# Retention, routed experts and a second MLP on one core: VectorE's steps beside the experts emitted later, and a weight conversion with two outputs

## The chip, the cores and the metric

The kernel runs on one NeuronCore of a Trainium2 chip. TensorE (PE; PEld is its weight load) does the matrix products and transposes, VectorE (DVE) and ScalarE (ACT) work element by element, GpSimd (POOL) issues gathers and scatters and large copies, SyncE (SP) issues the other DMAs. Each engine works through its own list of instructions in the order in which the program emitted them, and waits on semaphores for the others. The metric is the device time of one execution in microseconds (us), as the median of several.

## The reference

Three stages follow one another. The weights of the last stage come as 64-bit numbers.

```python
scores = scale * np.matmul(q, k.transpose(0, 1, 3, 2))        # 8 batches, 8 heads, 576 x 64
ret = scores * Dmat[None, :, :, :]                            # gamma ** (i - j) below the diagonal
x = np.matmul(ret, v)  ...  .reshape(4608, 512)

logits = x @ w_gate                                           # 8 experts, each takes 576 tokens
for idx in np.argsort(-logits.flatten()):
    tok, e = (int(idx) // E, int(idx) % E)
    if assigned[tok] >= 0 or counts[e] >= cap:
        continue
    assigned[tok] = e
    counts[e] += 1
for e in range(E):
    out[mask] = np.maximum(x[mask] @ w1[e], 0.0) @ w2[e]      # 512 -> 1024 -> 512

h = x @ w_in                                                  # 512 -> 2048 -> 512, all 4608 tokens
g = h * np.clip(h + 3.0, 0.0, 6.0) / 6.0
out = g @ w_out
```

## The kernel before

**Stages.** The retention stage and the logits come first, and the routing of the first expert follows. From 187.8 us on `mlps` runs two MLPs as one stream of TensorE work: the experts (eight times 576 tokens, in two halves of 288), then the second MLP (12 blocks of 384 tokens). The experts are filled one after the other: routing `r` finds which expert is full next and which 576 tokens it takes, by eight counting steps, a sort and a decoding.

**Arithmetic.** Every operand is split into a high and a low part, so that a product is three matmuls (`mm3`). For each weight, each token column and each hidden value there is thus a copy to the high part on ScalarE and a subtraction for the low part on VectorE. In an expert's half, unit `f` has 12 matmuls of the first layer (`A`, into one of two PSUM buffers `h`) and 12 of the second (`Bm`); `A(u+2)` is emitted ahead of `Bm(u)`. An expert is 384 matmuls. Unit `A(u+2)` writes the PSUM buffer that ScalarE (L724) and VectorE (L725) read for `A(u)`, and 36 matmuls lie between.

**What sets the order.** The order is written by the program itself. `mm3` calls `tick` after each matmul, and `tick` lets the side jobs go on that were started with `spawn`; a side job emits some instructions and says with `yield n` after how many further matmuls it wants to go on. The numbers are those of `PARAMS`. The side jobs are
- `route`: the next routing. In each counting step VectorE compares (L367, tile `cmp`), TensorE counts (L373), ScalarE copies (L377, `gs`), TensorE adds up (L382), VectorE tests (L385, `ge`), TensorE sums the flags (L389). At the end a sort (L456, L461) and a decoding that gives the list of tokens (L504, `idx`), with `self.routed` counted up behind it; the next routing begins at once (L510 to L367).
- `weights`: gathers w1 and w2 of the known expert (L530, issued by POOL) and splits them (L544 on ACT, twice L549 on DVE).
- `xload`: gathers the token rows (L567, issued by POOL), transposes them on TensorE (L592, PSUM bank `tp`, five pieces for each expert) and splits them (L596, L597). `w_xg` is how many matmuls lie between the issue of the first gather and its transposes.
- `convert`: turns the 64-bit weights of the second MLP into high and low parts. It goes through 32 pieces of 128x512 numbers: a load by SP (L615, one buffer `c_raw`), seven steps on VectorE (L633 to L657) and three on ScalarE (L642, L645, L653), and a store to HBM by SP (L620). All pieces write the same output buffer `self.cvo` (a part of `big`), and the store of piece `i-1` is emitted with the fourth step of piece `i`, one step ahead of L652, which writes the buffer again.
- `w2load`: brings the converted weights back, 2 MB at a time, into the buffers of the expert weights that are free (L672, issued by POOL).
- `yload`: brings the experts' results (stored by SP, L745) to the second MLP.

Before a unit of TensorE is emitted, `need_x`, `need_w` and `run_until` make the side jobs emit all that this unit reads.

## Time and profile before

| | us |
|---|---|
| median of 3 runs (1524.6 to 1533.34) | 1532.13 |
| the profiled execution | 1529.34 |
| its span | 1527.6 |
| PE busy, PEld busy | 1440.0, 1316.4 |
| DVE busy, ACT busy, POOL busy | 701.8, 530.9, 232.4 |
| experts, from 187.8 to 716.3 | 528.5 |

The profiled execution is 1.7 us longer than its span, the part that the instructions' records don't cover. Busy time alone says little here: VectorE is busy for 46% of the span, but it has its work between 150 and 720 us and little after that.

### The profile page before, as it was taken

Reading aid. Unit: us, or ns where it says so; the run is one execution under the profiler, and the core shown is the slowest. Engines: PE = TensorE matmul, PEld = TensorE weight load, DVE = VectorE, ACT = ScalarE, POOL = GpSimd, SP = SyncE. Lnnn points to the kernel's source line nnn. Section 1 sums busy time; section 2 is a strip of 40 time slices with the busy share of each in tenths; the row PEclk is TensorE's granted clock in tenths of the full one; section 3 lists DMA queues with packets and bytes.
Section 4 is the critical chain, followed back from the end, with each engine's and each line's share of the span. In section 5 each row is a group of like instructions: output and inputs, shape, how many; then the busy total and the mean of one; then the engine's idle time right before and its main releaser. Section 6 shows DMA issues by size and latency. Waiting matters only on the chain.

```text
span 1527.6 us, 27247 instructions
## 1 busy us (share of the span) xinstructions
PE 1440.0 (94%) x11270; PEld 1316.4 (86%) x11270; DVE 701.8 (46%) x1723; ACT 530.9 (35%) x1033; POOL 232.4 (15%) x260
## 2 busy tenths in 40 slices
PE   6898598889999899989999999999999999999998
PEld 5677488888989889989899999999999999999997
DVE  3344577678778686754232323233232323323222
ACT  3233343443434435533232323233232323323222
POOL 6860212121131122100000000000000000000000
PEclk9999798999999999999999999999999999999999
DMA  9981734455454457668410101000010100000000
GB/s 360 380 316 51 244 102 143 134 188 173 154 173 152 150 184 230 200 245 285 167 37 16 42 1 42 15 28 27 16 38 4 42 12 30 27 16 32 1 21 21
DMA packets 62988, 171.81 MB, mean 112 GB/s; under 512 B 7696, under 2 KB 22288, under 8 KB 61840
## 3 DMA queue, kind: packets, MB, share of 16 engines
q1 hardware_dynamic: 43568, 96.09, 18.1%
q0 software_dynamic: 16464, 70.26, 14.0%
q10 hardware_dynamic: 2832, 3.72, 0.7%
q8 instruction: 88, 1.44, 0.4%
q14 instruction: 36, 0.29, 0.1%
HBM read 124.96 MB, written 45.09 MB: 111 GB/s over the span
## 4 chain that ended last, share of the span: by engine, by line
issue 50%; PE 3%; POOL 3%; POOLq 0%; DVE 0%
POOL out_dram L790 2%; PE h L703 2%; PE y L703 1%; POOL nop L796 0%; POOLq L929 0%; POOL big L672 0%; POOLq L790 0%; POOL pair L672 0%; DVE hg L725 0%; POOLq L672 0%
## 5 line engine op out<-in xcount | busy, mean ns | idle before, releaser
L763 DVE SCALAR_TENSOR_TENSOR r<-r,h 128x384 f32<-128x384 f32 x192 | 106.4, 554 | 449.1 <-ACT r L762 449.1
L703 PE MATMUL h<-big,pair 128*128 128x288 f32 (+1 forms) x1440 | 281.6, 316 | 7.1 <-DVE hg L725 6.4
L762 ACT ACTIVATE r<-h,bias 128x384 f32<-128x384 f32 x192 | 111.5, 581 | 441.8 <-PE h L703 433.8
L703 PEld LDWEIGHTS h<-big,pair 128*128 128x128 f32 x1440 | 223.9, 194 | 10.3 <-DVE hg L725 6.7
L703 PE MATMUL h<-big 128*128 128x288 f32 (+1 forms) x864 | 188.6, 323 | 0.6 <-ACT big L596 0.6
L703 PE MATMUL y<-hg,pair 128*128 128x288 f32 x1056 | 172.3, 305 | 2.1 <-ACT r L744 2.1
L703 PE MATMUL h<-yact,big 128*128 128x384 f32 x768 | 173.4, 337 | 0.2 <-DVE r L763 0.2
L703 PE MATMUL h<-yact,pair 128*128 128x384 f32 x768 | 173.3, 337 | 0.0
L766 DVE TENSOR_TENSOR hg<-r,hg 128x384 fp32r<-128x384 f32 x192 | 107.3, 559 | 113.4 <-ACT hg L765 113.4
L703 PEld LDWEIGHTS y<-hg,pair 128*128 128x128 f32 x1056 | 150.3, 192 | 2.8 <-ACT r L744 2.4
L790 POOL DMA_INDIRECT out_dram<-xg,idx x36 | 35.1, 975 | 761.8 <-ACT xg L789 755.3
L780 PE MATMUL y<-pair,hg 128*128 128x512 f32 x576 | 148.9, 394 | 0.0
L780 PE MATMUL y<-big,hg 128*128 128x512 f32 x576 | 148.9, 394 | 0.0
L703 PEld LDWEIGHTS h<-yact,big 128*128 128x128 f32 x768 | 138.4, 188 | 6.9 <-DVE r L763 0.6
L703 PEld LDWEIGHTS h<-big 128*128 128x128 f32 x864 | 141.2, 194 | 3.3 <-ACT big L596 0.8
L703 PEld LDWEIGHTS h<-yact,pair 128*128 128x128 f32 x768 | 138.3, 188 | 6.1
L765 ACT ACTIVATE hg<-r 128x384 fp32r<-128x384 f32 x192 | 100.7, 524 | 119.1 <-DVE r L763 119.1
L530 POOL DMA_INDIRECT raw<-in_w_dram,widx x65 | 65.9, 1015 | 395.6 <-DMA xn<-raw 57.8
L780 PEld LDWEIGHTS y<-big,hg 128*128 128x128 f32 x576 | 106.7, 188 | 16.8
L780 PEld LDWEIGHTS y<-pair,hg 128*128 128x128 f32 x576 | 106.7, 188 | 16.6
L724 ACT ACTIVATE hg<-h 128x288 fp32r<-128x288 f32 x128 | 52.0, 409 | 115.6 <-PE h L703 111.1
L725 DVE SCALAR_TENSOR_TENSOR hg<-h,hg 128x288 fp32r<-128x288 f32 x128 | 58.2, 454 | 50.7 <-ACT hg L724 49.5
(171 smaller groups left out, 1766.6 us busy)
## 6 DMA issues: line engine op xcount, KB each, us to landing
qk<-in_qk_dram SPq DMA_DIRECT2D x36, 512.0 KB, 6.9
kv<-in_kv_dram SPq DMA_DIRECT2D x32, 512.0 KB, 7.1
c_raw<-in_w_dram SPq DMA_DIRECT2D x32, 512.0 KB, 4.0
w<-big SPq DMA_DIRECT2D x32, 512.0 KB, 4.9
yr<-yT SPq DMA_DIRECT2D x48, 192.0 KB, 2.3
pair<-w POOLq DMA_DIRECT2D x4, 2048.0 KB, 10.0
big<-w POOLq DMA_DIRECT2D x4, 2048.0 KB, 12.2
yT<-r SPq DMA_DIRECT2D x32, 144.0 KB, 3.9
```

The lines of the kernel that those rows point to most:

```text
L530: nc.gpsimd.indirect_dma_start(out=raw, out_offset=None, in_=a[("w1", "w2")[w]], in_offset=bass.IndirectOffsetOnAxis(ap=self.widx[:, r, g: ...
L703: self.nc.tensor.matmul(out, w, x, start=(first and i == 0), stop=(last and i == 2))
L724: nc.scalar.activation(h[:, 0], p, AF.Relu)
L725: nc.vector.scalar_tensor_tensor(h[:, 1], p, 0.0, h[:, 0].bitcast(F32), op0=OP.max, op1=OP.subtract)
L762: nc.scalar.activation(r, p, AF.Relu, bias=self.bias[:, 0:1])
L763: nc.vector.scalar_tensor_tensor(r, r, 6.0, p, op0=OP.min, op1=OP.mult)
L765: nc.scalar.activation(g[:, 0], r, AF.Copy)
L766: nc.vector.tensor_tensor(g[:, 1], r, g[:, 0].bitcast(F32), OP.subtract)
L780: nc.tensor.matmul(acc[b][t], g[:, gw, x], w[:, ww, c:c + 512], start=(f == 0 and i == 0), stop=(f == 15 and i == 2))
L790: ins = nc.gpsimd.indirect_dma_start(out=a["out"], out_offset=bass.IndirectOffsetOnAxis(ap=self.idx[:, 3 * b + t:3 * b + t + 1], axis=0), ...
```

## The change

The change has these parts (line numbers are those of the program before):
- **Steps behind their inputs.** VectorE's low part of a hidden value (L725) is put in a list (`later`) and emitted 5 matmuls after the ScalarE step that it reads. The low parts of token columns come `w_low` = 5 matmuls after ScalarE's, and VectorE's `ge` and the next `cmp` come `w_pe` = 2 matmuls after TensorE's steps that they read.
- **Spacing.** The first counting step of routings 2 to 7 has 34 matmuls between `cmp` and its use instead of 22 (`w_first` + 4 `add`); `add` is -1 instead of 0 for routings 0 and 1. Token pieces of experts 1 to 3 are emitted with 11 matmuls between one and the next for the first three (`w_xt0`), and expert 2's first transposes come 36 instead of 50 matmuls after the gather's issue (`w_xg` for `r` < 3).
- **Conversion.** It begins after routing 1 instead of at the start of the experts. It has two output buffers in turn, and the store is emitted right behind the last step of its piece. A piece has 7 times 17 matmuls (before 7 times 16) while routings go on, and 3 times 6 and 4 times 9 (before 7 times 10) after that. The order of the pieces is `CONV`; those of the first two eighths come last, and are written straight into two weight buffers that expert 6 was the last to use, without a store and a load.
- The decoding waits with `tp_x` until the token pieces under way have been read from the bank `tp`.

```diff
-PARAMS = dict(w_first=18, w_cmp=12, w_hop=7, w_hop2=8, w_pre=22, w_dec=16, w_add=1, w_t=2, w_load=40, w_gran=16, w_half=10, w_gran0=24,
-              w_xg=36, w_xg2=50, w_xt=40, w_cv=16, w_cv2=10, n_nat=12)
+PARAMS = dict(w_first=30, w_cmp=11, w_hop=5, w_hop2=7, w_pe=2, w_low=5, w_pre=22, w_dec=16, w_add=1, w_t=2, w_load=40, w_load0=60, w_gran=16, w_half=8, w_gran0=24, w_gran1=10,
+              w_xg=36, w_xg2=50, w_xt=40, w_xt0=4, w_cv=17, w_cv2=6, w_cv3=9, n_nat=12)
+CONV, DIRECT = (2, 3, 4, 5, 6, 7, 0, 1), 2
...
+    def later(self, n, do):
+        self.due.append([n, do])
...
     def tick(self, n=1):
+        for x in self.due:
+            x[0] -= n
+        while self.due and self.due[0][0] <= 0:
+            self.due.pop(0)[1]()
...
-            add = self.w_add if r > 1 else 0
+            add = self.w_add if r > 1 else -1
...
+                        if r:
+                            yield self.w_pe
                         ge = rw.tile([128, E], F16, name="ge")
...
+            while self.tp_x:
+                yield 1
             self.tp_busy = True
...
-                yield self.w_xg if r < 2 else self.w_xg2
+                yield self.w_xg if r < 3 else self.w_xg2
...
+            for src, d in parts:
                 nc.scalar.activation(d[:, 0], src, AF.Copy)
+            if r:
+                yield self.w_low
+            for src, d in parts:
                 nc.vector.tensor_tensor(d[:, 1], src, d[:, 0].bitcast(F32), OP.subtract)
...
-            yield self.w_xt
+            yield self.w_xt0 if r < 4 and j < 2 else self.w_xt
...
+        while self.routed < 2:
+            yield 1
+        nxt = issue(0)
         yield 30
+        for i, (g, w, hf) in enumerate(seq):
+            raw, o = nxt, self.cvo[i % 2]
+            if i >= direct:
+                while self.pB < (self.w2_old[g] // 4) * 16 + 8 + 2 * (self.w2_old[g] % 4) + 2:
+                    yield 1
+                o = self.pairs[SLOT[g]][:, w, :, hf * n:hf * n + n]
...
-            if i > first:
-                store(i - 1)
-            if i + 1 < last and self.cv_bufs == 1:
-                issue(i + 1)
-            yield pace()
-            o = self.cvo
+            if i + 1 < len(seq):
+                nxt = issue(i + 1)
+            yield pace(True)
...
             V.tensor_tensor(o[:, 1], t0.bitcast(F32), ta, OP.mult)
-            yield pace()
-        store(last - 1)
+            if i < direct:
+                nc.sync.dma_start(self.w32[g, :, w, :, hf * n:hf * n + n], o.bitcast(F32))
+            self.converted = i + 1
+            yield pace(True)
...
+    def need_w2(self, f, w):
+        k, direct = CONV.index(f // 2), len(CONV) - DIRECT
+        self.run_until("convert", lambda: self.converted >= (4 * k + 2 + 2 * w if k >= direct else 4 * k + 4))
+        if k < direct:
+            self.run_until("w2load", lambda: self.w2_ready > k)
...
-            nc.vector.scalar_tensor_tensor(h[:, 1], p, 0.0, h[:, 0].bitcast(F32), op0=OP.max, op1=OP.subtract)
+            self.later(self.w_low, lambda: nc.vector.scalar_tensor_tensor(h[:, 1], p, 0.0, h[:, 0].bitcast(F32), op0=OP.max,
+                                                                          op1=OP.subtract))
```

In the lists that follow, before and after, a line's number is that of its own program: L652, L657, L615, L620, L725, L745 of before are L671, L676, L639, L678, L747, L768 of the change.

The first place is SP's list from the end of expert 6 on, before. `w<-big` is the store of a converted piece, `c_raw` the load of the next, `yT` the experts' results.

```order
L620 DMA w_77<-big 128x2x512
L615 DMA c_raw<-in_w_dram 128x1024
L745 DMA yT<-r 128x288 x2
L745 DMA yT<-ys 128x288 x2
L620 DMA w_77<-big 128x2x512
L615 DMA c_raw<-in_w_dram 128x1024
L620 DMA w_77<-big 128x2x512
L615 DMA c_raw<-in_w_dram 128x1024
L620 DMA w_77<-big 128x2x512
L615 DMA c_raw<-in_w_dram 128x1024
L745 DMA yT<-r 128x288 x2
L745 DMA yT<-ys 128x288 x2
```

The same in the change, from the last store of a piece on.

```order
L678 DMA w_77<-big 128x2x512
L639 DMA c_raw<-in_w_dram 128x1024
L678 DMA w_77<-big 128x2x512
L639 DMA c_raw<-in_w_dram 128x1024
L768 DMA yT<-r 128x288 x2
L768 DMA yT<-ys 128x288 x2
L639 DMA c_raw<-in_w_dram 128x1024 x4
L768 DMA yT<-r 128x288 x2
L768 DMA yT<-ys 128x288 x2
L639 DMA c_raw<-in_w_dram 128x1024 x2
L768 DMA yT<-r 128x288 x2
L768 DMA yT<-ys 128x288 x2
```

The store stood behind the four result stores of a half expert and now stands ahead of them; the last eight pieces have no store, and their loads follow one another.

The second place is VectorE's list where routing 3 begins, before (`v`, `t`, `ky`, `K`, `oh` lead to the first `cmp`; `big<-c_ta` and `c_t` are the conversion).

```order
L341 TENSOR_REDUCE v<-L 128x36 [waits DVE_49]
L347 MEMSET cmp 128x32
L349 TENSOR_SCALAR t<-v 128x36 [waits DVE_49]
L652 SCALAR_TENSOR_TENSOR big<-c_ta,c_t_4156 128x512 [waits DMAHW6_49,Activation_49]
L352 TENSOR_TENSOR ky<-t,v 128x36 [waits DVE_49]
L354 TENSOR_SCALAR t<-ky 128x36 [waits DVE_49]
L356 CAST K_4351<-t 128x36 [waits DVE_49]
L357 TENSOR_SCALAR ky<-ky 128x36
L725 SCALAR_TENSOR_TENSOR hg<-h,hg 128x288 [waits Activation_49]
L359 TENSOR_TENSOR oh<-L,v 128x288
L361 CAST K_4360<-ky 128x36 [waits DVE_49]
L367 SCALAR_TENSOR_TENSOR cmp<-K_4351,cf 128x576
```

The same in the change.

```order
L353 TENSOR_REDUCE v<-L 128x36 [waits DVE_49]
L359 MEMSET cmp 128x32
L361 TENSOR_SCALAR t<-v 128x36 [waits DVE_49]
L364 TENSOR_TENSOR ky<-t,v 128x36 [waits DVE_49]
L567 TENSOR_TENSOR pair_2217<-raw,pair_2217 128x512 [waits DMASW3_49,Activation_49]
L366 TENSOR_SCALAR t<-ky 128x36 [waits DVE_49]
L368 CAST K_4300<-t 128x36 [waits DVE_49]
L369 TENSOR_SCALAR ky<-ky 128x36
L371 TENSOR_TENSOR oh<-L,v 128x288
L373 CAST K_4306<-ky 128x36 [waits DVE_49]
L379 SCALAR_TENSOR_TENSOR cmp<-K_4300,cf 128x576
```

L725 and L652 stood within the chain to `cmp`; now a weight split (L567) stands there, and L747 is behind `cmp`.

The third place is TensorE's list from the decoding of routing 2 on (which is the row ahead of the first one here), before; `h` and `y` are expert 1, `rt<-oh,cmp` the first count of routing 3.

```order
L703 MATMUL y_4219<-hg,big 128x288
L703 MATMUL y_4220<-hg,big 128x288 x3
L703 MATMUL y_4221<-hg,big 128x288 x3
L703 MATMUL y_4222<-hg,big 128x288 x3
L703 MATMUL h<-big,pair_2214 128x288 x12
L703 MATMUL y_4219<-hg,big 128x288 x3
L703 MATMUL y_4220<-hg,big 128x288 x3
L703 MATMUL y_4221<-hg,big 128x288 x3
L703 MATMUL y_4222<-hg,big 128x288 x3
L703 MATMUL h<-big,pair_2214 128x288 x12
L703 MATMUL y_4219<-hg,big 128x288
L373 LDWEIGHTS cmp
```

The same in the change, from the 34th matmul behind the decoding on.

```order
L725 MATMUL y_4187<-hg,big 128x288 x3
L725 MATMUL y_4188<-hg,big 128x288 x3
L725 MATMUL h<-big,pair_2214 128x288 x6
L610 MATMUL tp<-ident,xg 128x128 x4
L725 MATMUL h<-big,pair_2214 128x288 x6
L725 MATMUL y_4185<-hg,big 128x288 x3
L725 MATMUL y_4186<-hg,big 128x288 x2
L610 MATMUL tp<-ident,xg 128x128 x4
L725 MATMUL y_4186<-hg,big 128x288
L725 MATMUL y_4187<-hg,big 128x288 x2
L385 LDWEIGHTS cmp
L385 MATMUL rt<-oh,cmp 128x64
```

From the decoding to the first count there were 47 matmuls of the expert, and now there are 59; ahead of the count now stand two pieces of expert 2's token transposes (`tp<-ident,xg`), the first of them 45 matmuls behind the decoding.

## Rows read from the trace of the kernel before

**Rows 1.** Windows by expert: us, busy by engine, clock, DMA share, GB/s.

```profile
187.80:263.50 75.70, 68.20 (x561) 64.28 (x562) 54.91 (x167) 28.71 (x57) 15.24 (x15) 0.91 0.39 129
263.50:338.30 74.80, 65.23 (x570) 61.81 (x569) 53.39 (x159) 30.82 (x63) 14.69 (x15) 0.93 0.50 157
338.30:405.10 66.80, 62.35 (x567) 59.71 (x565) 52.26 (x158) 28.56 (x59) 13.65 (x14) 0.97 0.52 166
...
538.90:599.00 60.10, 57.49 (x447) 56.29 (x447) 48.23 (x158) 26.43 (x50) 18.49 (x18) 0.97 0.63 201
599.00:655.80 56.80, 54.67 (x402) 54.43 (x401) 39.99 (x78) 30.99 (x56) 10.58 (x11) 0.97 0.67 215
655.80:716.30 60.50, 54.09 (x387) 53.85 (x386) 28.79 (x56) 20.91 (x42) 2.16 (x5) 0.94 0.73 259
1000.00:1100.00 100.00, 100.00 (x503) 90.68 (x502) 30.32 (x56) 30.23 (x57) 3.25 (x6) 1.00 0.07 23
```

**Rows 2.** The waits of PE: us in total, times, longest.

```profile
PE rt L373 <- DVE cmp L367: 17.2, 11, 3.5
...
PE h L703 <- DVE hg L725: 6.4, 1, 6.4
...
PE rt L382 <- ACT gs L377: 4.9, 1, 4.9
...
PE tp L592 <- DMA xg<-xn,idx: 3.5, 2, 3.2
```

**Rows 3.** The timeline of DVE at three places: start, us, what, idle before.

```profile
277.35 0.69 DVE L652 SCALAR_TENSOR_TENSOR big<-c_ta,c_t 128x512 fp32r<-128x512 f32 x1 [5.80 <-DMA w<-big]
...
515.79 0.69 DVE L652 SCALAR_TENSOR_TENSOR big<-c_ta,c_t 128x512 fp32r<-128x512 f32 x1 [3.28 <-DMA w<-big]
...
673.01 0.69 DVE L652 SCALAR_TENSOR_TENSOR big<-c_ta,c_t 128x512 fp32r<-128x512 f32 x1 [9.70 <-DMA w<-big]
```

**Rows 4.** The timeline of SP ahead of the last of them.

```profile
659.39 0.88 SPq L745 DMA_DIRECT2D yT<-ys  x2
660.36 0.43 SPq L620 DMA_DIRECT2D w<-big  x1
```

**Rows 5.** All stores of the conversion (line L620).

```profile
DMA to landing us min/median/max: 2.7/4.9/12.6
```

**Rows 6.** The chain that ended last, after 675 us: start, us, what.

```profile
675.21 3.25 PE h L703 x12
678.46 2.23 PE y L703 x12
...
682.29 1.60 PE y L703 x12
```

**Rows 7.** The timeline where routings 3 and 4 begin.

```profile
315.55 0.22 DVE L504 SCALAR_TENSOR_TENSOR idx<-g,tp 128x4 int32<-128x4 f32 x2
...
319.78 0.74 DVE L367 SCALAR_TENSOR_TENSOR cmp<-K,cf 128x576 f16<-128x576 f32 x1
...
320.58 0.32 PE L373 MATMUL rt<-oh,cmp 128*128 128x64 f16 x5 [3.46 <-DVE cmp L367]
...
381.04 0.32 PE L373 MATMUL rt<-oh,cmp 128*128 128x64 f16 x5 [3.19 <-DVE cmp L367]
```

**Rows 8.** The timeline where expert 1's tokens come in.

```profile
243.65 0.35 DVE L504 SCALAR_TENSOR_TENSOR idx<-g,tp 64x1 int32<-64x1 f32 x2
...
248.79 0.63 PE L592 MATMUL tp<-ident,xg 128*128 128x128 f32 x4 [3.24 <-DMA xg<-xn,idx]
```

**Rows 9.** DVE by line in expert 6: busy us, mean ns, idle before.

```profile
L725 DVE SCALAR_TENSOR_TENSOR hg<-h,hg 128x288 fp32r<-128x288 f32 x17 | 7.8, 456 | 9.4 <-ACT hg L724 9.4
...
L657 DVE TENSOR_TENSOR big<-c_t,c_ta 128x512 fp32r<-128x512 f32 x6 | 4.1, 687 | 0.1
...
L640 DVE TENSOR_SCALAR c_t<-c_raw 128x512 int32<-128x512 int32 x6 | 2.5, 418 | 0.0
```

**Rows 10.** All loads of the conversion (line L615).

```profile
DMA to landing us min/median/max: 3.6/4.0/6.2
```

More of the change, by code (lines that the diff above doesn't have):

```diff
@@ L121, in step, with flush @@
             del self.side[name]
+    def later(self, n, do):
+        self.due.append([n, do])
+    def flush(self):
+        while self.due:
+            self.due.pop(0)[1]()
     def tick(self, n=1):
+        for x in self.due:
+            x[0] -= n
+        while self.due and self.due[0][0] <= 0:
+            self.due.pop(0)[1]()
         for name in list(self.side):
@@ L601, in xload, with convert @@
                     yield from issue(u)
-            yield self.w_xt
-    def convert(self, first, last):
+            yield self.w_xt0 if r < 4 and j < 2 else self.w_xt
+    def convert(self):
         nc, a, cv = self.nc, self.a, self.cv_p
@@ L608, in convert, with pace @@
         s0 = 0x38100000 / 2.0
-        raws = {}
-        seq = [(g, w, hf) for g in range(8) for w in range(2) for hf in range(2)]
+        seq = [(g, w, hf) for g in CONV for w in range(2) for hf in range(2)]
+        direct = 4 * (len(CONV) - DIRECT)
         def issue(i):
             g, w, hf = seq[i]
-            raw = cv.tile([128, n, 2], I32, name="c_raw", bufs=self.cv_bufs)
+            raw = cv.tile([128, n, 2], I32, name="c_raw")
             nc.sync.dma_start(raw, a["w64"][g, :, w, hf * n:hf * n + n].bitcast(I32).rearrange("p (n t) -> p n t", t=2))
-            raws[i] = raw
-        def store(i):
-            g, w, hf = seq[i]
-            nc.sync.dma_start(self.w32[g, :, w, :, hf * n:hf * n + n], self.cvo.bitcast(F32))
-            self.converted = i + 1
-        def pace():
-            return self.w_cv if "route" in self.side else self.w_cv2
-        issue(first)
-        yield 30
-        for i in range(first, last):
-            g, w, hf = seq[i]
-            raw = raws.pop(i)
+            return raw
+        def pace(late=False):
+            return self.w_cv if "route" in self.side else self.w_cv3 if late else self.w_cv2
+        while self.routed < 2:
+            yield 1
+        nxt = issue(0)
+        yield 30
+        for i, (g, w, hf) in enumerate(seq):
[4 more added lines that the diff above has]
+                o = self.pairs[SLOT[g]][:, w, :, hf * n:hf * n + n]
             lo, hi = raw[:, :, 0], raw[:, :, 1]
@@ L633, in convert @@
             V.tensor_scalar(t0, hi, 3, 0x3FFFF000, op0=OP.logical_shift_left, op1=OP.bitwise_and)
+            ta = cv.tile([128, n], F32, name="c_ta")
+            nc.scalar.activation(ta, hi, AF.Abs, bias=self.bias[:, 1:2])
             yield pace()
             V.scalar_tensor_tensor(t0, hi, -0x40000000, t0, op0=OP.bitwise_and, op1=OP.bitwise_or)
-            if i + 1 < last and self.cv_bufs == 2:
-                issue(i + 1)
+            nc.scalar.activation(ta, ta, AF.Abs, bias=self.bias[:, 2:3])
             yield pace()
@@ L657, in convert @@
             V.tensor_tensor(o[:, 1], t0.bitcast(F32), ta, OP.mult)
-            yield pace()
-        store(last - 1)
+            if i < direct:
+                nc.sync.dma_start(self.w32[g, :, w, :, hf * n:hf * n + n], o.bitcast(F32))
+            self.converted = i + 1
+            yield pace(True)
     def w2load(self):
-        old = (26, 27, 28, 29, 30, 31)
-        for g in range(8):
-            while self.converted < 4 * g + 4:
+        for k, g in enumerate(CONV[:len(CONV) - DIRECT]):
+            while self.converted < 4 * k + 4:
@@ L771, in Dm @@
             _, b, _, f = u
+            if b == 0:
+                self.need_w2(f, 1)
             w = self.pairs[SLOT[f // 2]][:, 1]
@@ L880, in run @@
                          for i in range(3)]
-            self.cvo = big[:, 15104:16128].rearrange("p (a b) -> p a b", a=2)
+            self.cvo = [big[:, 15104 + 1024 * i:16128 + 1024 * i].rearrange("p (a b) -> p a b", a=2) for i in range(2)]
             for name in ("xload", "w2load", "yload"):
```

41 lines of the change are left out of this document (18 added, 23 removed).

## The prediction

> **What bounds the kernel now.** I read the windows by expert first, then PE's waits, then the timeline on both sides of each long wait. The second MLP needs no reading beyond one row: between 1000 and 1100 us PE is busy all the time at full clock [rows 1], and the change leaves its instructions as they are. What can move lies in the experts, 528.5 us. There 12 matmuls take 1.60 us at full clock [rows 6], 0.133 us each, so the 384 of an expert take 51.2 us. The windows [rows 1] have 75.7 and 74.8 us for experts 0 and 1, 66.8 for expert 2 (3 and 4 are within 0.2 of it), 60.1, 56.8 and 60.5 for 5, 6 and 7. Some 8 us of each of the first five are the routing's own matmuls and the transposes, an estimate: expert 2 has 165 PE instructions more than expert 6 and is 10 us longer, waits included. The rest, some 75 us over all eight, is waiting, and PE at the lower of its two clocks (1.2 instead of 2.4 GHz) behind the waits: a mean clock of 0.93 over 74.8 us says that some 10 us ran at the lower one, and 0.97 says 4 us in each of the middle experts.
>
> PE waits mostly for VectorE [rows 2]: 17.2 us for the first count of a step (`cmp`), 6.4 once for a low part of `h`, 4.9 once for ScalarE's `gs`; 3.5 for gathered tokens. VectorE is busy for 52.3 of expert 2's 66.8 us [rows 1], and its list is strict, so what holds one step holds all behind it. Two things hold it. One is the store of the conversion: L652 writes the only output buffer and waited 5.80, 3.28 and 9.70 us for the store to land [rows 3]. The other is its own backlog where a routing ends and the next begins: in the 5 us behind `idx` at 315.55 it works without a pause and `cmp` comes at 319.78, while PE has waited 3.46 us for it [rows 7].
>
> **The change, part by part.**
>
> *Stores (term 1).* All three waits follow one pattern. The store is behind the four result stores on SP, and those wait for the expert's half to end: the result stores go out at 659.39, the piece's store at 660.36, and it lands 12.6 us later at worst [rows 4, 5]. PE's share of the three waits is 4.9 (behind `gs`), 1.9 (at 517 us, a part of the 17.2) and 6.4 us [rows 2], together 13.2. Behind the third the clock costs more: 24 matmuls took 3.25 and 2.23 us instead of twice 1.60 [rows 6], so 2.3 us. Expert 1 shows as much lost clock [rows 1], so I take the same 2.3 behind the first. After the change the store is ahead of the result stores, and the next piece writes the other buffer; L652 then waits for a store that is two pieces, 108 matmuls or 14.4 us, older, against 12.6 at worst. The last eight pieces have no store. Term 1 is -(13.2 + 4.6) = -17.8 us. Next late in these places is VectorE's ordinary backlog, which the change doesn't raise in the first two; bounds -8 (a third wait as long as the first comes back in expert 7) to -18.
>
> The Trainium skill ("DMA: Bandwidth & Descriptors", Anatomy of one DMA) gives a fixed 2.0 us and 436 GB/s for a transfer, an estimate of 3.2 us for a store of 512 KB. By that the store of 660.36 would have landed before L652 came to it, the second buffer would be worth some 2 us of PE's time, and the sum would end 16 us higher. The row's 9.70 us speaks against it here, so the sum keeps term 1.
>
> *Spacing of the first count (term 2).* The count stands 59 instead of 47 matmuls behind the decoding, 12 times 0.133 or 1.6 us. It can give that at each of four starts of a routing; two of the waits are 3.46 and 3.19 us [rows 7], and the 17.2 us less 1.9 leave 8.7 for the other two and the small ones. But expert 2's tokens take the place at the first of the four. In the trace tokens are transposed 4.8 us after the end of `idx` at the earliest (244.0 to 248.8) [rows 8], so with `idx` done at 315.8 not before 320.6, which is when PE goes on now. The first transposes now stand 36 matmuls, 4.8 us, behind the emission of `idx`, and PE passed that point at 312.1 (320.58 less the wait of 3.46, less 38 matmuls). It would come to them at 316.9 and wait 3.7. So the first start gives nothing. At the other three, tokens and count stand together 50 matmuls behind `idx`, and the wait falls by 1.6 each: 4.8. The clock fell behind each of them (0.97 of 67 us is 4 us, 2 us lost). Whether it still falls behind a wait of half the length no row here says: 0 to 1.7 each, and I take half of 5. Term 2 is -7.4, bounds 0 to -12.
>
> *Expert 0 (term 3).* Conversion starts after routing 1, so VectorE has three of its steps less in the stretch that ends with `idx` at 243.65: two of 0.68 and one of 0.42 [rows 9], some 1.6 us. PE's wait of 3.24 [rows 8] goes to 1.6. A clock of 0.91 over 75.7 us [rows 1] is 13.6 us at the lower level; the 4 at the start stay, the rest costs 4.8 now and I take half of it off. Term 3 is -4.0, bounds 0 to -8.
>
> *Steps behind their inputs.* VectorE stands idle 9.4 us before L725 in expert 6 alone [rows 9], waiting for ScalarE. With five matmuls between, other steps fill that. PE doesn't wait for these directly, so I count nothing; the gain shortens the backlogs of terms 2 and 3 and is what lets the bounds there reach further. The price: L725 must be done 36 matmuls or 4.8 us behind its unit, and 0.7 of that are now gone before it is emitted.
>
> *Denser conversion (term 4).* A piece is four steps of 0.68 us and three of 0.42 [rows 9], 4.0 us. After the routings it is spread over 54 instead of 70 matmuls, so expert 6 gets up to 1.6 pieces more, 6 us on a VectorE that is busy for 40.0 of 56.8 us [rows 1] and idle for ScalarE in most of the rest. If it fits in the idle time it costs nothing, if not 6; nearest is expert 2, where VectorE at 78% comes with a wait of 3.19 us [rows 7]. I take +3 for experts 5 to 7, bounds 0 to +8. The change also shifts two pieces from expert 0 to the end; expert 7 has the room, with 28.8 of 60.5 busy.
>
> *The load behind the result stores (term 5).* With one `c_raw`, the late pace leaves 36 matmuls, 4.8 us, between a load's issue and its first reader; loads land in 4.0 (3.6 to 6.2) us [rows 10]. Two loads of this stage are emitted 9 and 3 matmuls behind four result stores, which SP issues only after the half has ended, two of them in 0.88 us [rows 4]. VectorE then stands 3 us or so, twice, and 4.1 us of slack remain before PE feels it: +1, bounds 0 to +6.
>
> *Token pieces close together (term 6).* Experts 2 and 3 get their first three pieces 11 matmuls, 1.5 us, apart through one PSUM bank, while transposing (0.6) and two readers (0.6 each) take 1.8. Before, two of them were forced together anyway. +1.5, bounds 0 to +6.
>
> The two loads and eight stores of 2 MB eighths that fall away, and POOL's list, cost nothing, since PE waits for none of it now.
>
> **Sum.** -17.8 - 7.4 - 4.0 + 3 + 1 + 1.5 = -23.7. Against the profiled execution's 1529.34 that is 1505.6; the three runs shown lie from 1524.6 to 1533.3 with a median of 1532.1, 2.8 above it. I forecast 1506 us.
>
> **Rivals.**
> *The backlog takes it back.* VectorE remains as full as it is, PE's waits at the starts only change their names (tokens for count), the clock falls as before, and terms 4 to 6 come to half their upper bounds. Only the stores count: -17.8 + 9 (terms 4 to 6 to some 10 of 20) = -8.8, 1520 us. For it: VectorE at 78% through expert 2, and the tokens of expert 2 as worked out. Against: VectorE's 9.4 us of idle time that the later emission opens. Chance 0.22.
>
> *The waits are of one piece.* If a shorter backlog also keeps the clock up, experts 0 to 4 come near 62 us each (51.2, 8 and 3 for what waits remain). They take 351 us now, so that is -41; with -8.7 for the third store and terms 4 to 6 it makes -44, 1485 us. For it: the clock is lost only behind waits. Against: the tokens at 36 matmuls. Chance 0.15.
>
> *The last loads are late.* The direct pieces must be done when the second MLP reads them, with one `c_raw` in series: a piece takes a load and the 2.2 us up to its last read of `c_raw`. The last three loads run while the 2 MB copies fill the DMA engines. At 6.2 us a load eight pieces take 67 us, and the last is needed 480 matmuls or 64 us after expert 7 begins: harmless. If three loads took as long as the longest store and longer, PE would wait at the start of the second MLP: five pieces at 8.4 and three at L + 2.2 exceed 64 us, and the gain of 24 too, from L = 13 us on; at L = 19, half as much again as the longest store, 42 us of waiting and 3 of clock make 1551 us. Against: no load took over 6.2 us [rows 10], and before too some ran beside such copies; for: a store took 12.6 [rows 5]. Chance 0.06. The Trainium skill ("DMA: Bandwidth & Descriptors", Issuing engines are not separate DMA queues) says that DMAs of SP and POOL end on the same 16 engines and interleave. By that the loads would suffer like the stores, 1551 us; the trace's loads agree with it less than its stores do.
>
> *The buffer isn't what was waited for.* If SP's order alone held the stores, the second output adds nothing; since the change mends both, the time would be the same 1506.
>
> **How the numbers follow.** My forecast, 1498 to 1517, has 0.54; the rivals 0.22, 0.15 and 0.06, and 0.03 is for what I don't see. Faster by over 1%, about what a measurement of this kernel can tell from no change, means under 1517: all of the second rival and nearly all of the forecast, 0.68. Within 1% is the first rival and the forecast's edge, 0.25; slower by over 1% is the third rival, 0.07. The range takes in the first rival with its costs at two thirds and the second nearly: 1488 to 1529.
>
> **What would show it.** In the profile after: no wait of VectorE for `w<-big` over 1 us (term 1); expert 1 under 67 us and expert 7 under 54; PE's waits for `cmp` under 8 us, but tokens (`tp<-xg`) above the 3.5 of now, with one wait of 3 us or so near the start of routing 3 (term 2); a clock above 0.95 in experts 0 and 1 (term 3); expert 6 no longer than 59 us (term 4). The forecast is wrong if PE waits for VectorE as long as before in other places (then 1520), or if PE stands at the start of the second MLP for the direct pieces.

## The result, and the profile after

The changed kernel takes 1512.32 us (median of 5 runs, 1507.79 to 1517.24), the kernel before 1531.17 in the same comparison. The ratio is 0.9889, 95% interval 0.9855 to 0.9923: faster by 1.1%. The profiled execution took 1507.79 us (span 1505.8). It is the fastest of the five, so sums from the profile come out 4.5 us better than the median.

By stage (us, from the windows; the last two columns are the experiments e1 and e11 below):

| | before | after | e1 | e11 |
|---|---|---|---|---|
| experts begin at | 187.8 | 185.9 | 189.9 | 189.8 |
| expert 0 | 75.7 | 70.8 | 72.0 | 71.6 |
| expert 1 | 74.8 | 69.6 | 68.9 | 66.3 |
| experts 2 to 4 | 200.6 | 186.8 | 201.3 | 191.0 |
| expert 5 | 60.1 | 58.8 | 58.5 | 58.3 |
| expert 6 | 56.8 | 59.2 | 53.0 | 53.4 |
| expert 7 | 60.5 | 54.5 | 58.8 | 58.7 |
| all experts | 528.5 | 499.7 | 512.5 | 499.3 |
| second MLP to the end of the span | 811.3 | 820.2 | 811.6 | 813.1 |

So the experts gave 28.8 us, and the second MLP took 8.9 of them back.

The windows of the kernel after by expert (columns as in [rows 1]): experts 0, 1, 2, then 6, 7 and the start of the second MLP.

```profile
185.90:256.70 70.80, 64.23 (x569) 60.42 (x570) 47.22 (x152) 24.05 (x50) 16.89 (x15) 0.97 0.34 110
256.70:326.30 69.60, 62.81 (x567) 59.85 (x565) 52.97 (x158) 31.05 (x64) 14.53 (x15) 0.98 0.53 173
326.30:389.00 62.70, 61.04 (x563) 58.11 (x561) 49.31 (x152) 28.94 (x59) 15.21 (x15) 1.00 0.54 171
...
571.90:631.10 59.20, 54.94 (x407) 53.53 (x406) 42.26 (x82) 29.22 (x56) 10.40 (x11) 1.00 0.67 220
631.10:685.60 54.50, 52.21 (x386) 51.73 (x385) 34.24 (x67) 25.51 (x47) 1.95 (x4) 1.00 0.52 179
685.60:715.00 29.40, 23.61 (x108) 20.82 (x107) 9.72 (x18) 9.28 (x19) 1.59 (x3) 0.88 0.81 315
```

The clock column is 1.00 from expert 2 to expert 7, where it was 0.94 to 0.97 [rows 1]. In the last row PE is busy for 23.6 of 29.4 us at a clock of 0.88: that is the new loss.

VectorE's output step by line, after (busy us, mean ns, idle before it; L671 is L652 of before):

```profile
L671 DVE SCALAR_TENSOR_TENSOR big<-c_ta,c_t 128x512 fp32r<-128x512 f32 x24 | 16.4, 684 | 0.0
L671 DVE SCALAR_TENSOR_TENSOR pair<-c_ta,c_t 128x512 fp32r<-128x512 f32 x8 | 5.5, 685 | 0.0
```

It never waits for a store; the three waits of [rows 3] are gone. The waits of PE, after:

```profile
PE rt L403 <- DVE ge L399: 8.8, 19, 0.8
...
PE y L725 <- ACT r L767: 5.6, 3, 2.2
...
PE h L725 <- DVE r L785: 3.2, 2, 2.9
...
PE tp L610 <- DMA xg<-xn,idx: 3.1, 3, 1.6
PE y L804 <- ACT r L767: 2.6, 1, 2.6
...
PE h L725 <- DVE hg L747: 0.9, 2, 0.7
PE rt L385 <- DVE cmp L379: 0.2, 1, 0.2
```

The 17.2 us for `cmp` [rows 2] are 0.2. In their place stand many waits under 1 us for `ge` (8.8 us in all, before 4.1), and waits for result copies (L767), 5.6 and 2.6 us in all, where the list of before had 2.1 once.

The timeline where routing 3 begins, after:

```profile
304.61 0.22 DVE L522 SCALAR_TENSOR_TENSOR idx<-g,tp 128x4 int32<-128x4 f32 x2
...
308.40 0.75 DVE L379 SCALAR_TENSOR_TENSOR cmp<-K,cf 128x576 f16<-128x576 f32 x1
...
308.95 0.63 PE L610 MATMUL tp<-ident,xg 128*128 128x128 f32 x4 [1.60 <-DMA xg<-xn,idx]
...
312.47 0.66 PE L610 MATMUL tp<-ident,xg 128*128 128x128 f32 x4 [1.45 <-DVE big L620]
...
313.36 0.32 PE L385 MATMUL rt<-oh,cmp 128*128 128x64 f16 x5
```

`cmp` ends 4.2 us before PE needs it. The tokens cost 1.60 and then 1.45 us of waiting, where 3.46 us went for the count [rows 7].

The timeline at the start of the second MLP, after (`big<-w` is a 2 MB copy of `w2load`):

```profile
675.93 0.66 POOL L688 DMA_DIRECT2D big<-w  x1 [5.83 <-PE y L725]
...
677.26 0.33 SPq L639 DMA_DIRECT2D c_raw<-in_w_dram  x1
...
687.13 0.77 ACT L659 ACTIVATE c_ta<-c_raw,bias 128x512 f32<-128x512 int32 x1 [6.25 <-DMA c_raw<-in_w_dram]
...
694.73 1.12 SPq L768 DMA_DIRECT2D yT<-r  x2
694.76 3.91 PE L804 MATMUL y<-pair,hg 128*128 128x512 f32 x9 [2.63 <-ACT r L767]
...
704.50 0.58 ACT L784 ACTIVATE r<-h,bias 128x384 f32<-128x384 f32 x1 [8.39 <-DMA yT<-r]
...
705.72 0.69 PE L725 MATMUL h<-yact,big 128*128 128x384 f32 x1 [2.89 <-DVE r L785]
```

The window in which the last load was under way, after (columns as in [rows 1]):

```profile
677.30:687.10 9.80, 9.80 (x69) 9.80 (x68) 2.35 (x5) 1.42 (x3) 0.53 (x1) 1.00 0.93 332
```

Two things follow one another here. The last load of the conversion is issued at 677.26 and has landed only at 687.13, 9.9 us later, while the DMA engines were busy for 0.93 of the time, and everything on ScalarE behind its first reader is late: the result copies of expert 7 (L767), and with them PE, which waits 2.63 us. The store of these results then goes out at 694.73, and ScalarE at L784 wants its buffer `r` again: 8.39 us, of which PE feels 2.89. The nine matmuls behind the first wait take 3.91 us; they run at the lower clock.

### The profile page after: what moved, and what is told of

It is laid out like the page before. It is cut to its first block, busy times and chain, and to the rows that moved or that the text cites. A ratio compares the mean times of both kernels' runs of the same rounds, so it can differ in the third digit from the quotient of the medians.

```text
span 1505.8 us, 27252 instructions
## 1 busy us (share of the span) xinstructions
PE 1428.6 (95%) x11270; PEld 1304.7 (87%) x11270; DVE 700.5 (47%) x1723; ACT 530.7 (35%) x1033; POOL 235.2 (16%) x257
## 4 chain that ended last, share of the span: by engine, by line
issue 52%; PE 3%; POOL 3%; DMA 2%; ACT 1%; DVE 1%; POOLq 0%; SPq 0%; ACTq 0%
POOL out_dram L814 2%; PE y L725 2%; PE h L725 2%; DMA c_raw<-in_w_dram 1%; DMA raw<-in_w_dram,widx 1%; ACT c_ta L659 0%; POOL nop L820 0%; DVE c_t L667 0%; ACT big L562 0%; ACT c_ta L662 0%; ACT c_ta L672 0%; DVE big L567 0%; DVE big L620 0%; ACT hg L746 0%; ACT pair L562 0%
## 5 line engine op out<-in xcount | busy, mean ns | idle before, releaser
L725 PE MATMUL h<-big,pair 128*128 128x288 f32 (+1 forms) x1440 | 277.5, 312 | 1.4 <-DVE hg L747 0.9
L784 ACT ACTIVATE r<-h,bias 128x384 f32<-128x384 f32 x192 | 111.5, 581 | 441.4 <-PE h L725 429.4
L725 PEld LDWEIGHTS h<-big,pair 128*128 128x128 f32 x1440 | 218.8, 190 | 6.8 <-DVE hg L747 1.8
L725 PE MATMUL h<-big 128*128 128x288 f32 (+1 forms) x864 | 183.9, 317 | 0.3 <-DVE big L620 0.2
L725 PE MATMUL h<-yact,big 128*128 128x384 f32 x768 | 174.7, 339 | 2.9 <-DVE r L785 2.9
L725 PE MATMUL h<-yact,pair 128*128 128x384 f32 x768 | 173.4, 337 | 0.3 <-DVE r L785 0.3
L725 PE MATMUL y<-hg,pair 128*128 128x288 f32 x1056 | 167.1, 300 | 3.4 <-ACT r L767 3.4
L725 PEld LDWEIGHTS y<-hg,pair 128*128 128x128 f32 x1056 | 146.8, 188 | 5.2 <-ACT r L767 3.8
L725 PEld LDWEIGHTS h<-yact,big 128*128 128x128 f32 x768 | 139.7, 189 | 9.6 <-DVE r L785 3.3
L725 PEld LDWEIGHTS h<-yact,pair 128*128 128x128 f32 x768 | 138.5, 188 | 6.7 <-DVE r L785 0.5
L725 PEld LDWEIGHTS h<-big 128*128 128x128 f32 x864 | 137.1, 188 | 3.1 <-DVE hg L747 0.5
L548 POOL DMA_INDIRECT raw<-in_w_dram,widx x64 | 68.8, 1075 | 367.2 <-issue 62.7
L725 PE MATMUL y<-hg,big 128*128 128x288 f32 x480 | 77.1, 303 | 2.2 <-ACT r L767 2.2
```

Of the source, the lines that this page charges most:

```text
L548: nc.gpsimd.indirect_dma_start(out=raw, out_offset=None, in_=a[("w1", "w2")[w]], in_offset=bass.IndirectOffsetOnAxis(ap=self.widx[:, r, g: ...
L725: self.nc.tensor.matmul(out, w, x, start=(first and i == 0), stop=(last and i == 2))
L784: nc.scalar.activation(r, p, AF.Relu, bias=self.bias[:, 0:1])
```

## The experiments

**e1, e2, e3: the stores alone.** Three kernels made from the one before: with two outputs and the early store, with the early store alone, with two outputs alone.

```diff
-            self.cvo = big[:, 15104:16128].rearrange("p (a b) -> p a b", a=2)
+            self.cvo = [big[:, 15104 + 1024 * i:16128 + 1024 * i].rearrange("p (a b) -> p a b", a=2) for i in range(2)]   # e1, e3
-            if i > first:
-                store(i - 1)
...
             V.tensor_tensor(o[:, 1], t0.bitcast(F32), ta, OP.mult)
+            store(i)   # e1, e2
```

Both edits, e1. 

> The kernel before with two output buffers for the conversion in turn and each store emitted right behind the last step of its piece; nothing else of the change. Theory 1 (the stores): the three waits of VectorE for a store cost PE 13 us and the clock 4.6, so this alone takes 13 to 18 us off before, to 1513 to 1518 us, in experts 1, 4 and 7 only, and no wait of VectorE for a store over 1 us is left. Rival (the backlog): VectorE is full around the start of each routing, a store's wait only moves into the next backlog, and less than 6 us are gained, 1525 us or more.

The early store alone, e2. 

> The kernel before with the store emitted right behind the last step of its piece, still with one output buffer. If SP's order alone held the stores (the store behind four result stores), this gains as much as the version with two buffers, within 3 us. If the buffer counts, the store of a late piece, 40 matmuls or 5.3 us ahead of the step that writes the buffer again, still holds VectorE in expert 7, where a store took 12.6 us: some 7 us of wait stay there, and the gain is some 9 us, half of the other.

Two outputs alone, e3. 

> The kernel before with two output buffers in turn, the store where it was, with the fourth step of the next piece. If the buffer counts, the step that writes a buffer comes a whole piece later than before (70 to 112 matmuls, 9 to 15 us) and no wait for a store over 1 us is left: the same 13 to 18 us as with both. If SP's order counts, waits of 2 us and more stay behind the ends of the halves.

Measured: 1512.94 us, ratio 0.9886 (0.9859 to 0.9913); 1514.31, 0.9895 (0.9865 to 0.9924); 1514.24, 0.9887 (0.9852 to 0.9921). The three can't be told apart, and none of them from the whole change.

The total is that of theory 1, but the place isn't. By stage, e1's gain of 16.0 us lies in expert 1 (-5.9), experts 0 and 6 (-3.7, -3.8), 5 and 7 (-1.6, -1.7); experts 2 to 4 are as before (201.3 against 200.6). Expert 7, with the longest of the three waits, gives only 1.7 us, and its windows in e2 and e3 are 59.0 and 57.7 us. VectorE no longer waits there for a store in e1, but as long for a load (`pair<-w` is a 2 MB copy):

```profile
647.22 0.55 POOL L670 DMA_DIRECT2D pair<-w  x1 [3.62 <-PE y L701]
...
650.44 0.33 SPq L615 DMA_DIRECT2D c_raw<-in_w_dram  x1
...
663.03 0.43 DVE L633 TENSOR_SCALAR c_t<-c_raw 128x512 int32<-128x512 int32 x1 [9.40 <-DMA c_raw<-in_w_dram]
...
663.88 3.25 PE L701 MATMUL h<-big,pair 128*128 128x288 f32 x12 [4.16 <-DVE hg L723]
```

In e2, with one buffer, it is the store again, 15.13 us on its way in the chain that ended last:

```profile
643.98 15.13 DMA w<-big
```

```profile
659.21 0.69 DVE L650 SCALAR_TENSOR_TENSOR big<-c_ta,c_t 128x512 fp32r<-128x512 f32 x1 [7.87 <-DMA w<-big]
...
661.40 3.25 PE L701 MATMUL h<-big,pair 128*128 128x288 f32 x12 [4.72 <-DVE hg L723]
```

In e3 it is a load, with 8.33 us of VectorE and 3.21 of PE. So either edit mends the stores of experts 1 and 4, where no wait for one is left in any of the three; in expert 7 neither does, since there a transfer of the conversion is late beside the 2 MB copies, whichever it is. What the change does beside the stores is worth nothing in the sum, and yet the stages of the change and e1 differ by 12.8 us in the experts: gains and losses of the same size.

**e4: no direct pieces.** The change with the pieces in their natural order, all stored and loaded.

```diff
-CONV, DIRECT = (2, 3, 4, 5, 6, 7, 0, 1), 2
+CONV, DIRECT = (0, 1, 2, 3, 4, 5, 6, 7), 0
```

> The changed kernel with the pieces in their natural order and all of them through HBM, none written straight into a weight buffer. The change loses some 9 us at the start of the second MLP (820 us from there to the end instead of 811). Theory D (the direct pieces): the weights used first are converted last, so this brings 7 to 9 us back, 1504 us. Theory L (loads and result stores among the 2 MB copies): what holds ScalarE there is the last load of the conversion and the result stores, both still emitted beside the copies, so no more than 3 us come back; the eight stores more may cost up to 3 us: 1510 to 1515 us.

Measured: 1511.27 us, ratio 0.9907 (0.9873 to 0.9941), no different in the sum. The second MLP takes 811.2 us again instead of 820.2, but expert 7 takes 62.3 instead of 54.5. The timeline of e4 there (SP, ScalarE, PE):

```profile
640.70 0.33 SPq L639 DMA_DIRECT2D c_raw<-in_w_dram  x1
...
652.67 0.76 ACT L659 ACTIVATE c_ta<-c_raw,bias 128x512 f32<-128x512 int32 x1 [8.27 <-DMA c_raw<-in_w_dram]
...
654.27 2.72 PE L725 MATMUL h<-big,pair 128*128 128x288 f32 x12 [4.12 <-DVE hg L747]
```

A load of 12.0 us, in another place: in e4, as in e1, the first two copies are issued where expert 7 begins (636.28 and 639.36), and in the change 38 and 45 us into it (669.54 and 675.93). The new order of the pieces didn't make the loads slow; it moved the late load, with the copies, from expert 7 to the second MLP.

**e5, e6, e7: the end of the experts.** e5 puts the loads of the last five pieces into freed weight buffers, two under way at a time; e6 writes half of expert 7's last results from other buffers; e7 does both.

```diff
+            if i >= 27:
+                raw = self.raw_p.tile([128, 1024], F32, name="raw").bitcast(I32).rearrange("p (n t) -> p n t", t=2)   # e5, e7
...
+            for u in ((i + 1,) if i < 25 else (26, 27) if i == 25 else (i + 2,)):
...
+                    if r == E - 1 and hb and d < 2:
+                        o = self.xg_p.tile([128, DM], F32, name="xg")   # e6, e7
```

> The change, with the loads of the last five pieces put into weight buffers that have come free, so that two loads are under way at a time instead of one. Theory A (the second MLP begins late because the last loads are in series beside the 2 MB copies): the 6 us waits of VectorE and ScalarE for c_raw at 687 go, PE's wait of 2.6 us and the half clock behind it too; the second MLP is 3 to 6 us shorter, 1507 us. Rival B (the copies slow every load, and two loads beside them only share the same rate): the last load lands as late as before, the second MLP stays at 820 us, 1512 us.

> The change, with half of the last results of expert 7 written from other buffers, so that the first hidden tile r of the second MLP doesn't reuse a buffer whose store to yT is still on its way. Theory A (ScalarE's 8.4 us wait for that store is a separate cost): PE's 2.9 us wait and the half clock behind it go, the second MLP is 3 to 6 us shorter, 1508 us. Rival B (the store only shows what the late load has already cost: PE is held by the pieces anyway): under 1 us changes, 1512 us.

> Both of the last two edits. Theory A: the two waits are separate and follow one another, so the gains add: the second MLP comes back from 820 to 812 us, the time to 1503 us, ratio 0.983 to the kernel before. Rival B (one of the waits covers the other): no more than the better of the two single edits.

Measured: 1506.08 us, ratio 0.9877 (0.985 to 0.9904); 1506.51, 0.9869 (0.9837 to 0.99); 1502.43, 0.9841 (0.9811 to 0.987). The kernel before was at 1527.49 in this comparison, so the ratios say less than the medians: 0.1%, 0.2% and 0.5% better than the change, each within the intervals. The stages say it more clearly: the second MLP takes 815.2, 816.1 and 810.7 us against 820.2. In e5 PE's wait of 2.6 us for the result copies is gone, in e6 2.2 of the 2.9 us for `r`, and in e7 PE waits for neither. The gains add, as theory A has it: two waits one behind the other, each worth 4 to 5 us.

**e8: low parts at once.** The change, with the low parts of hidden values and token columns emitted as before.

```diff
-            if r:
-                yield self.w_low
...
-            self.later(self.w_low, lambda: nc.vector.scalar_tensor_tensor(h[:, 1], p, 0.0, h[:, 0].bitcast(F32), op0=OP.max,
-                                                                          op1=OP.subtract))
+            nc.vector.scalar_tensor_tensor(h[:, 1], p, 0.0, h[:, 0].bitcast(F32), op0=OP.max, op1=OP.subtract)
```

> The change with the low parts of hidden values and token columns emitted at once, as in the kernel before, and all else as in the change. My prediction priced the steps behind their inputs at 0. Theory A (they are what keeps experts 2 to 4 at full clock, at 62 us each instead of 67): experts 2 to 4 go back to 65 to 67 us, 1522 us or more. Rival B (the spacing of first count and tokens does it): experts 2 to 4 stay within 1 us each, 1512 to 1514 us.

Measured: 1524.22 us, ratio 0.9978 (0.9957 to 1.0). Nearly all of the change is gone with this one part. (Without the `yield` the token pieces also stand 6 matmuls apart instead of 11; e11 leaves them alone.) Experts 1 and 2 go from 69.6 and 62.7 to 75.6 and 67.1 us at clocks of 0.91 and 0.97; experts 3 and 4 only to 63.3 both, so there the rival is half right. The timeline of e8 in expert 1 shows how:

```profile
273.23 1.06 ACT L562 ACTIVATE pair<-raw 128x1024 fp32r<-128x1024 f32 x1 [4.00 <-DMA raw<-in_w_dram,widx]
...
274.62 0.46 DVE L745 SCALAR_TENSOR_TENSOR hg<-h,hg 128x288 fp32r<-128x288 f32 x1 [4.55 <-ACT hg L744]
...
275.50 0.76 DVE L379 SCALAR_TENSOR_TENSOR cmp<-K,cf 128x576 f16<-128x576 f32 x1
...
276.31 0.45 PE L385 MATMUL rt<-oh,cmp 128*128 128x64 f16 x5 [3.45 <-DVE cmp L379]
```

VectorE stands 4.55 us before one low part because ScalarE is late with the high part, having stood 4.00 us for a gathered weight; `cmp`, which could have run long before, is behind it, and PE waits 3.45 us for `cmp`. ScalarE's lateness becomes VectorE's.

**e9: spacing undone.** The change with `w_first=18`. With `add` at -1 this also moves the first count of routing 1, which runs beside expert 0: it has 14 matmuls here, 26 in the change and 18 in the kernel before.

> The change with the spacing of the first count undone: 22 matmuls between cmp and its use as before, instead of 34; all else as in the change. Theory A (steps behind their inputs alone removed the long waits of experts 1 and 2, the spacing adds little): experts 2 to 4 stay within 1 us of 62.8, 61.8 and 62.3, 1512 to 1514 us. Rival B (my term 2: the spacing gives 1.6 us and some clock at each start of a routing): PE's waits for cmp come back with 1.5 to 3 us each in experts 1 to 4, 1518 to 1522 us.

Measured: 1516.9 us, ratio 0.99 (0.9878 to 0.9923), against 0.9889 for the change: unclear. The waits for `cmp` come back, as the rival has it. PE's waits in e9:

```profile
PE rt L385 <- DVE cmp L379: 11.3, 6, 3.3
```

The profiled execution, the slowest of six (1522.98), has experts 1 to 4 at 274.0 us against 256.4 (experts 2 to 4 at 201.4, as before the change), but expert 0 is 4.5 shorter and expert 7 2.8. In the sum the spacing is worth the 1.7 us between the ratios or some more. For experts 2 to 4 it seems worth more than that, and routing 1's longer first count seems to cost in expert 0; no run takes these two apart, and the sizes stay open.

**e10: token pieces apart again.** The pieces stand 47 matmuls apart here (40 in the kernel before), since the other yields of the change remain.

```diff
-                yield self.w_xg if r < 3 else self.w_xg2
+                yield self.w_xg if r < 2 else self.w_xg2
...
-            yield self.w_xt0 if r < 4 and j < 2 else self.w_xt
+            yield self.w_xt
```

> The change with the token pieces as before: 50 matmuls from the gather to the first transposes of expert 2, and 47 matmuls between pieces. Theory A (my term 6: close pieces cost a little and expert 2's early ones wait for the gather, 1.9 and 1.7 us in expert 1): expert 1 becomes 1 to 4 us shorter, 1509 to 1512 us. Rival B (pieces spread out are forced later, when the next routing is under way, and stand in its counts' way): experts 1 to 3 become longer by 2 us or more each, 1518 us.

Measured: 1520.78 us, ratio 0.9939 (0.9915 to 0.9963), some 8 us slower than the change, though the intervals just meet. The rival has the sign right, but not the place: expert 0, where expert 1's tokens are transposed, goes from 70.8 to 76.7 us (clock 0.91 for 0.97), experts 1 and 2 by 0.7 and 2.3. In e10 the next pieces fall at 253.8 and 255.8 us, where in the change three are transposed by 249.8; just ahead of them PE waits 2.36 us for `ge` and VectorE 3.18 us for a weight's high part, for which ScalarE stood 2.68 us until the weight was gathered. Whether the pieces delay that weight wasn't taken apart.

**e11: stores and hidden low parts, nothing else.** e1 with one more part of the change.

```diff
-            nc.vector.scalar_tensor_tensor(h[:, 1], p, 0.0, h[:, 0].bitcast(F32), op0=OP.max, op1=OP.subtract)
+            self.later(5, lambda: nc.vector.scalar_tensor_tensor(h[:, 1], p, 0.0, h[:, 0].bitcast(F32), op0=OP.max,
+                                                                 op1=OP.subtract))
```

> The kernel before with two output buffers, the store right behind the last step (1512.9 us so far), and one more part of the change alone: the low part of a hidden value emitted 5 matmuls after ScalarE's step. Nothing else of the change. Theory A (this step alone ends VectorE's backlog): experts 1 to 4 fall from 69, 68, 67 and 66 to 62 to 64 us, 1498 to 1503 us, faster than the whole change, since the second MLP isn't late here. Rival B (it works only with the spacing and the other steps that were moved): at most 1 us for each expert, 1509 to 1513 us.

Measured: 1504.04 us, ratio 0.9823 (0.9798 to 0.9847), better than the whole change (the intervals don't meet). Theory A holds in the total; of its 62 to 64 us, experts 2 and 4 have 63.6 and 62.1, experts 1 and 3 are at 66.3 and 65.3. First e1, then e11: PE's waits for `cmp`, and VectorE's low part of hidden values between 330 and 400 us (busy, mean ns, idle before it).

```profile
PE rt L373 <- DVE cmp L367: 15.6, 10, 3.6
...
L723 DVE SCALAR_TENSOR_TENSOR hg<-h,hg 128x288 fp32r<-128x288 f32 x17 | 7.8, 456 | 5.7 <-ACT hg L722 5.4
```

```profile
PE rt L380 <- DVE cmp L374: 9.3, 9, 2.3
...
L730 DVE SCALAR_TENSOR_TENSOR hg<-h,hg 128x288 fp32r<-128x288 f32 x18 | 8.1, 451 | 0.2 <-ACT hg L729 0.2
```

VectorE's idle time before `hg` falls from 5.7 to 0.2 us, PE's waits for `cmp` by 6.3 (a wait of 1.5 us at one first count is now put down to the step beside it, L660, so the counts themselves gain 4.8). The four experts 1 to 4 gain 12.9 us (270.2 to 257.3). The rest fits the clock, as the windows of expert 2 show (e1, then e11):

```profile
330.80:398.90 68.10, 63.65 (x567) 60.91 (x565) 52.32 (x158) 28.39 (x59) 13.63 (x14) 0.95 0.53 163
```

```profile
327.70:391.30 63.60, 60.96 (x567) 58.27 (x565) 51.95 (x158) 28.56 (x59) 13.46 (x14) 1.00 0.56 175
```

**e12: the late pace shifted.** e7, with the same pieces but more time between a load and its first reader.

```diff
-              w_xg=36, w_xg2=50, w_xt=40, w_xt0=4, w_cv=17, w_cv2=6, w_cv3=9, n_nat=12)
+              w_xg=36, w_xg2=50, w_xt=40, w_xt0=4, w_cv=17, w_cv2=3, w_cv3=11, n_nat=12)
```

> The kernel with both edits to the end (1502.4 us so far), with the late pace of a conversion piece shifted: 4 times 11 and 3 times 3 matmuls instead of 4 times 9 and 3 times 6, so that a load has 44 instead of 36 matmuls, at the same number of pieces. Theory A (expert 6's extra 2 to 5 us are ScalarE standing behind a load of c_raw, ahead of the result copies that PE waits for): ScalarE's waits for c_raw in expert 6 fall from 10.7 to under 4 us, PE's for r from 4.5 to under 2.5, expert 6 from 58.4 to 55 or 56 us, 1499 to 1500 us. Rival B (VectorE and ScalarE are too full there with 54 matmuls a piece, wherever they stand): expert 6 stays at 58 us or more, 1502 us or more.

Measured: 1501.47 us, ratio 0.9805 (0.978 to 0.983), the fastest of all kernels here, though its interval meets those of e7 and e11. Expert 6 goes from 58.4 to 56.1 us, as theory A has it, expert 7 from 54.6 to 53.0. ScalarE's waits for `c_raw` in expert 6, e7 and then e12:

```profile
ACT c_ta L662 <- DMA c_raw<-in_w_dram: 10.7, 5, 2.8
```

```profile
ACT c_ta L662 <- DMA c_raw<-in_w_dram: 5.8, 4, 2.0
```

They fall by half, not under 4 us. PE's waits for `r` fall from 4.5 to 3.4 over the whole kernel, not under 2.5, and in expert 6 they are 2.3 us in both; what goes there is PE's wait of 1.2 us for low parts (`hg`). So expert 6 got shorter as theory A has it, but not by the path that it names. The kernels with the pace of the change have expert 6 at 57.9 to 60.6 us, one execution each, so the 56.1 stands clear of them by 1.8. That the loads are a part of what the denser conversion costs is likely, not shown; e1's 53.0 isn't reached.

## Why the prediction was right, and where not

The time forecast was 1506, the measured one 1512.3, within the range; the profile gives -21.8 us of span for the -23.7 of the sum. But the terms came out otherwise, and errors cancelled, so that the nearness of the total is in good part luck.

*Stores (term 1, -17.8).* Right in the total, in part by luck. Alone they are worth 16.0 us by e1's stages and 1.1% by three ratios. But of the 17.8, 8.7 were for the wait in expert 7, 7.2 for that in expert 1 and 1.9 for that in expert 4; e1 gave 1.7, 5.9 and 0.8 there, and 9.1 in experts 0, 5 and 6, for which I had no term. "All three waits follow one pattern" is where it failed: SP's order explains the first two, while the third store was late beside the 2 MB copies, and in e1 a load takes its place. In the whole change expert 7 gave 6.0, where the copies come later; e4, with them at its start again, has 62.3 us. The fourth rival is right for the time, one of the two edits being enough (e2, e3), but not for its reason in expert 7. The estimate of 3.2 us from the Trainium skill ("DMA: Bandwidth & Descriptors", Anatomy of one DMA) rests on a fit to transfers that POOL issues, and these stores are SP's; the quickest of them took 2.7 us, the one beside the copies 12.6 [rows 5]. The sum by it, 16 us higher, is refuted by e1 to e3.

*Steps behind their inputs (counted as nothing).* This is the step that failed. "PE doesn't wait for these directly, so I count nothing" is true and beside the point: PE waits for `cmp`, and `cmp` stands on VectorE's list behind a low part that waits for ScalarE (e8's 4.55 us). They are worth 12 us of the change (e8, with the low parts of token columns) and 9 us on top of the stores alone (e11, without). The 9.4 us of idle time [rows 9] were the price tag, and I read them as room.

*Spacing (term 2, -7.4).* Experts 2 to 4 gave 13.8 us, more than the 12 of its bound. How that splits isn't a sum of two terms: e11 gets 9.6 of them without any spacing, and in the change without the spacing (e9) all are gone in the execution profiled. The part about the clock was mis-sized: in the change the waits for `cmp` and with them the falls of the clock are gone from experts 2 to 4, where I took half of the loss. Expert 2's tokens cost 1.60 instead of 3.7 us, as VectorE came to `idx` sooner relative to PE and the tokens could be transposed 4.1 us behind it instead of 4.8; so tokens didn't rise over the 3.5 us of before (3.1), as I had expected.

*Expert 0 (term 3, -4.0).* It gave 4.9; expert 1, which I wanted under 67, stayed at 69.6, and e11 has 66.3. The first count of routing 1, which my list of the change left out, has 26 matmuls instead of 18; e9 points to a cost there.

*Denser conversion (term 4, +3).* Expert 6 took 59.2 us, 2.4 more than before and 6 more than e1, so the size was right. Density alone isn't the reason: e12 is 2.3 us shorter than e7 at the same density, with more time for the loads.

*The load behind the result stores (term 5, +1) and the rival of the last loads (which I called harmless at 6.2 us a load, though its own 67 us exceed the 64).* Here is the second failure. The 6.2 us at most [rows 10] left loads out: that answer counts only those whose landing the profile tells. In the kernel before, too, a load was late beside the 2 MB copies:

```profile
659.50 0.55 POOL L672 DMA_DIRECT2D pair<-w  x1 [3.68 <-PE y L703]
```

```profile
662.78 0.33 SPq L615 DMA_DIRECT2D c_raw<-in_w_dram  x1
```

The trace's record of this load's completions ends at 674.1, 11.3 us after the issue. It cost nothing there, because VectorE stood at the store of 660.36 until 673.01 [rows 3]. At the end of expert 7 in the change one took 9.9 us, in e4 one took 12.0 and in e1 12.6. I had asked only whether PE would wait for the piece itself. It waited for what stood behind the load's reader on ScalarE, the result copies, and then for a buffer whose store was late in turn: 8.9 us (e5 to e7). The Trainium skill ("DMA: Bandwidth & Descriptors", Issuing engines are not separate DMA queues) says that DMAs of SP and POOL end on the same engines and interleave; the load of 677.26, beside the 2 MB copies (DMA share 0.93), agrees.

*Token pieces (term 6, +1.5).* Wrong in sign: taking the pieces apart costs some 8 us (e10).

The second rival was right on its mechanism in experts 2 to 4 (62 us each, as it said) and wrong for experts 0 and 1. Together: -16 for the stores, -12.8 for the rest in the experts, +8.9 at the second MLP, -1.9 in the start of the experts, which the change leaves alone and which lies between 185.9 and 191.2 us over all the runs. Some parts of the change were never taken apart: the later counting steps (`w_cmp`, `w_hop`, `w_hop2`), the spacing of the weights (`w_half`, `w_load0`, `w_gran1`), and two ScalarE steps of the conversion that the change emits earlier in the piece.

## What to carry to other kernels

An engine's idle time before an instruction isn't free room if the instruction waits at the head of a strict list: ask who stands behind it. Beside the stores, one deferred step brought the experts to 499.3 us here (e11), and the whole change with its dozen tuned numbers to 499.7, so try the parts of a change one by one on the kernel before. A DMA's longest landing time holds for the stage and the transfers that the answer covers, so look what was left out of it; where the change moves a DMA beside other transfers, price the wait of everything behind that DMA's first reader, the copies and buffers of other work too.

## What the runs showed of the hardware

The price of a wait of PE jumps where the clock falls behind it. In e1 PE waited 3.60, 3.19, 2.70 and 2.46 us for the first counts of four routings, and behind each the granted clock was at the lower level (1.2 GHz) for 3.4 or 6.8 us. In e11 it waited 2.29, 1.52, 1.70 and 1.49 us at the same four places, and only the first had such a stretch behind it (3.4 us): 5.0 us of waiting less, and 12.9 us of time. The length of the wait alone doesn't tell it near 2 us: the kernel after has waits of 1.9, 1.4 and 2.2 us in experts 5 to 7 and no fall, but one of 1.7 us in expert 1 with a fall behind it (a mean clock of 0.76 from 274 to 281 us), and the kernel before has one of 2.1 us in expert 6 with a fall.

A load of 512 KB that lands in 3.6 to 6.2 us where [rows 10] tells it took 9.9 to 12.6 us beside 2 MB copies (before, e1, e4 and the change), and a store 12.6 (before) and 15.1 us (e2, issued at 643.98). The DMA engines were busy for 0.90 or more of the time that each was under way. Not every load beside a copy is late: the one of 669.69 in the change, issued right behind a first copy, took 5.0 us. No run left the copies out, so that they are the cause is argued from the place: the late transfers moved with them.
